# Rounding's last product and its stores on GpSimd, raw weights by SyncE, a PReLU share on ScalarE, four v products per block

## The chip, the cores and the metric

One core of a Trainium2 chip runs the kernel. The metric is the device time of one execution in microseconds (us); the program runs once per measurement, and lower is better.

## What is computed

Talking-heads attention on 4 blocks of 448 tokens with 12 heads, then a two-layer MLP with PReLU on the 1792 tokens that come out. The MLP's weights come as float64 and are rounded to float32 on the chip.

```python
scores = scale * np.matmul(q, k.transpose(0, 1, 3, 2))
scores = np.einsum('bhij,hg->bgij', scores, w_pre)
scores = scores - np.max(scores, axis=-1, keepdims=True)
attn = np.exp(scores)
attn = attn / (np.sum(attn, axis=-1, keepdims=True) + 1e-09)
attn = np.einsum('bhij,hg->bgij', attn, w_post)
x = np.matmul(attn, v).transpose(0, 2, 1, 3).reshape(B * S, H * D)
h = x @ w_in
out = (np.maximum(h, 0.0) + alpha * np.minimum(h, 0.0)) @ w_out
```

## The kernel before, in words

**Attention in steps.** The 448 query rows of a block (one of four batches of tokens) are cut into seven chunks of 60 rows and one of 30 (chunk 7). A chunk is cut into groups of 10 rows by 12 heads; two groups make a step, 90 steps in all, of which steps -1 to 26 are called the lead here. Step n issues, in this order (`step`, from line 567): the mixing of the scores over heads, `mix(n)` (L207), with the row maximum on VectorE (L209); SyncE's relays, copies from SBUF to SBUF that lay the scores of a coming step out by heads (L197, and L200 for the 30-row chunk, which needs twice as many), three steps ahead, into six buffers that a mixing must have read before; `norm(n-1)` on VectorE; a v product if one is due; `post(n-2)`, the second mixing, with 56 small matmuls (L240); the exponentials on ScalarE (L216); the q-k products of a later chunk (L179).

**v products.** `pv` (L263) multiplies the finished attention columns of one or two chunks by v in two halves, for each with 3 x 4 x 2 x 2 matmuls (less the empty ones, 84), evicts with a ScalarE copy (L269) and a VectorE addition (L270), and stores to the scratch `x2` in DRAM (L273). `PVS` lists the chunks of each batch: five per block before. A batch comes LAG + 1 = 3 steps behind its last group. There is one buffer per half of v; the next block's v is loaded when the last batch of a block is issued (L169, L170).

**Conversion.** `convert` (from line 287) rounds the float64 weights in 64 units of 128x384. `round_f64` (from line 50) has five VectorE operations per unit: the exponent's bits (L60), the mantissa's high part (L64), adding the low word (L65), the sign (L66) and the product (L67); GpSimd clamps and scales the exponent between (L61, L62). The last two operations of a unit are issued after the first three of the next. GpSimd fetches the raw words of unit i + 4 when unit i is through (L295, four buffers); the rounded unit is stored to the scratch `wsc` by SyncE (L305), a step later, by `flush`, which runs twice per step. The lead issues 6 of these operations per step, the steps after it 9 until all are done.

**MoE.** When a block's x is whole, `split_x` loads it (L450) and splits each of six tiles into two float32r parts on VectorE (L460, L461). `moe` runs the two layers in pairs of 128-wide pieces, paced by `moe_work` between the attention's operations; weights come back from `wsc` (L338), are split by a ScalarE cast (L346) and a GpSimd subtraction (L347), and multiplied (L400, L434). `prelu` evicts a piece with two VectorE operations (L354, L355), a ScalarE cast (L360) and a subtraction (L361); `add_out` sums the second layer on VectorE (L367, L369). The first block of MoE runs from step 27 on beside the rest of the conversion.

Every engine works through its own list in order, so an instruction that waits holds all that stand behind it on that engine.

Of the kernel before, what the change touches and what calls it, by code (L numbers as in the profile page):

```python
# [70 lines left out]
def talking_heads_prelu(ctx: ExitStack, tc: tile.TileContext, q, k, v, w_pre, w_post, mask, w_in, w_out, alpha, out):  # L71
# [182 lines left out]
    def pv(i, hx):  # L254
        b, r0, cn, base, _, nh = pvs[i]
        to = grab()
        for cl in range(3):
# [9 lines left out]
        dst = xe[:, :3 * cn].rearrange("p (c i u) -> p c i u", i=HI, u=nh)  # L267
        src = to[:, :, :3 * cn].rearrange("p r (c u i) -> p r c i u", i=HI, u=nh)
        nc.scalar.copy(dst, src[:, 0])  # L269
        nc.vector.tensor_tensor(dst, src[:, 1], dst, ALU.add)  # L270
        free(to)
        skip = max(0, 420 - r0) if r0 > 360 else 0
        later.append(lambda: nc.sync.dma_start(  # L273
            out=x2[3 * hx:3 * hx + 3, :, b * S + r0 + skip:b * S + r0 + cn].rearrange("c p i -> p c i"),
            in_=xe[:, :3 * cn].rearrange("p (c i) -> p c i", c=3)[:, :, skip:]))

# [10 lines left out]
    def convert():  # L287
        todo = [(f, x, c) for f in range(NFC) for x in range(2) for c in range(0, DM, CU)]
        raw_c = {}

        def fetch_c(i):
            if i < len(todo):
                f, x, c = todo[i]
                raw_c[i] = cvp.tile([128, CU], I64, tag="cr", bufs=4, name=f"cr{f}_{x}_{c}")
# [382 lines left out]
```

## Time and profile before

| what | us |
| --- | --- |
| median of 3 runs | 998.38 (993.72 to 1003.52) |
| the profiled execution | 997.95 |
| its span | 996.1 |
| TensorE busy in the span | 870.4 (87%) |
| VectorE busy | 622.5 (62%) |
| ScalarE busy | 427.2 (43%) |
| GpSimd busy | 488.3 (49%) |

The span runs from the first to the last instruction of the profiled execution. A busy share is a mean over stages: the lead up to 207 us, the first MoE block beside the conversion up to 389 us, and from there MoE and attention on TensorE. The granted clock is TensorE's, as a share of its higher level (2.4 GHz; the lower is 1.2).

### The profile page before, as it was taken

The page shows a single profiled execution, that of the slowest core. Times are in us where ns is not written, and L with a number is a line of the kernel's source. Part 1 is how long each engine was busy: PE and PEld are TensorE (multiplying, and loading weights), DVE is VectorE, ACT ScalarE, POOL GpSimd, SP SyncE. Part 2 cuts the span into 40 slices and gives each one's busy share as a digit, 9 for nine tenths or more (in the row PEclk, how much of TensorE's full clock was granted, in tenths as well). Part 3 has the DMA queues.
Part 4 walks back from the last instruction along what each step waited for, and adds up shares of the span by engine and source line. Part 5 has one row for each costly group of instructions (what it writes and reads, how often), then busy time and mean ns, then how long its engine had stood idle before and what let it go on. Part 6 is the DMA issues. An engine that isn't in the chain of part 4 may idle for free. (4 is left out here: it accounts for less than half of the span.)

```text
span 996.1 us, 28867 instructions
## 1 busy us (share of the span) xinstructions
PE 870.4 (87%) x12204; PEld 677.2 (68%) x12204; DVE 622.5 (62%) x1077; ACT 427.2 (43%) x780; POOL 488.3 (49%) x562
## 2 busy tenths in 40 slices
PE   6687667596897885997999989999999999999997
PEld 2354435464774763875777866877787888879997
DVE  3699766588799798554544445555654464654564
ACT  1466455243334342453554545443645454232231
POOL 6555534547556753452435424550633334467661
PEclk7799988787898897997999989999999999999999
DMA  7788968746666964464544554465534433544322
GB/s 182 242 255 250 249 184 266 246 144 195 191 181 188 260 188 137 132 195 135 152 122 134 139 122 134 126 176 190 156 119 120 125 99 92 155 130 124 111 80 72
DMA packets 79729, 161.81 MB, mean 162 GB/s; under 512 B 26276, under 2 KB 64304, under 8 KB 79600
## 3 DMA queue, kind: packets, MB, share of 16 engines
q0 software_dynamic: 21312, 90.58, 33.4%
q1 hardware_dynamic: 57432, 68.18, 20.9%
q8 instruction: 96, 1.57, 0.7%
q10 hardware_dynamic: 856, 1.21, 0.5%
q14 instruction: 33, 0.27, 0.1%
HBM read 97.62 MB, written 23.59 MB: 122 GB/s over the span
## 5 line engine op out<-in xcount | busy, mean ns | idle before, releaser
L347 POOL TENSOR_TENSOR ws<-wr,ws 128x768 fp32r<-128x768 f32 x128 | 237.2, 1854 | 300.0 <-ACT ws L346 297.9
L434 PE MATMUL p<-g,ws 128*128 128x448 f32 x1152 | 258.1, 379 | 16.9 <-ACT e L216 7.9
L400 PE MATMUL p<-xs,ws 128*128 128x448 f32 x1152 | 258.0, 377 | 5.2 <-DVE xs L460 3.7
L434 PEld LDWEIGHTS p<-g,ws 128*128 128x128 f32 x1152 | 221.5, 195 | 55.5 <-ACT e L216 9.6
L400 PEld LDWEIGHTS p<-xs,ws 128*128 128x128 f32 x1152 | 216.9, 192 | 48.5 <-issue 13.4
L209 DVE TENSOR_REDUCE nm<-p 128x2 f32<-128x896 f32 x90 | 97.6, 1084 | 105.3 <-PE p L207 105.1
L246 ACT COPY at<-p 128x960 f32<-128x960 f32 x88 | 86.7, 985 | 173.1 <-PE p L240 173.0
L216 ACT ACTIVATE e<-p,nm 128x448 f32<-128x448 f32 x180 | 112.6, 634 | 99.7 <-DVE nm L209 66.9
L240 PEld LDWEIGHTS p<-r,e 64*64 64x64 f32 x5040 | 105.7, 140 | 71.6 <-issue 43.7
L346 ACT CAST ws<-wr 128x768 fp32r<-128x768 f32 x128 | 103.9, 843 | 91.4 <-issue 58.5
L240 PE MATMUL p<-r,e 64*64 64x60 f32 x5040 | 111.1, 227 | 33.0 <-issue 12.2
L179 PE MATMUL p<-k,q 64*64 64x448 f32 x768 | 107.9, 606 | 34.8 <-DVE t L355 15.2
L369 DVE TENSOR_TENSOR acc<-p,acc 128x896 f32<-128x896 f32 x84 | 90.9, 1086 | 70.5 <-PE p L434 69.2
L207 PE MATMUL p<-sr,wk 64*64 64x448 f32 (+1 forms) x720 | 106.0, 596 | 16.5 <-DMA sr<-st 12.2
L354 DVE TENSOR_SCALAR t<-p,alpha_sb 128x448 f32<-128x448 f32 x64 | 43.4, 678 | 98.7 <-PE p L400 98.7
L263 PEld LDWEIGHTS p<-at,v 64*64 64x64 f32 x3360 | 88.0, 138 | 23.5 <-issue 19.6
L263 PE MATMUL p<-at,v 64*64 64x120 f32 (+2 forms) x3360 | 89.3, 253 | 12.8 <-DMA v<-in_v_dram 7.8
L183 ACT COPY st<-p 128x896 f32<-128x896 f32 x95 | 84.1, 913 | 34.2 <-DMA sr<-st 18.4
L338 POOL DMA_DIRECT2D wr<-wsc x128 | 72.2, 564 | 39.9 <-POOL ws L347 35.3
L207 PEld LDWEIGHTS p<-sr,wk 64*64 64x64 f32 (+1 forms) x720 | 26.7, 141 | 58.2 <-issue 28.6
L179 PEld LDWEIGHTS p<-k,q 64*64 64x64 f32 x768 | 28.3, 143 | 54.5 <-ACT st L183 18.1
L61 POOL TENSOR_SCALAR ce<-ce 128x384 int32<-128x384 int32 x64 | 34.4, 537 | 52.5 <-DVE ce L60 50.5
(47 smaller groups left out, 670.9 us busy)
## 6 DMA issues: line engine op xcount, KB each, us to landing
wr<-wsc POOLq DMA_DIRECT2D x128, 384.0 KB, 3.9
sr<-st SPq DMA_DIRECT2D x332, 105.0 KB
cr<-in_w_in_dram POOLq DMA_DIRECT2D x32, 384.0 KB, 5.0
cr<-in_w_out_dram POOLq DMA_DIRECT2D x32, 384.0 KB, 5.5
wsc<-ct SPq DMA_DIRECT2D x64, 192.0 KB
xr<-x SPq DMA_DIRECT2D x24, 224.0 KB
out_dram<-acc SPq DMA_DIRECT2D x12, 448.0 KB
q<-in_q_dram POOLq DMA_DIRECT2D x54, 90.0 KB, 4.9
```

Of the source, the lines that this page charges most:

```text
L179: nc.tensor.matmul(pt[64 * cc:64 * cc + 64, r, :S], q_t[ci][h, (3 * cc + p) * cn + SR0 * cc:(3 * cc + p) * cn + SR0 * cc + 64], k_t[b, p][ ...
L207: nc.tensor.matmul(to[hf:hf + 64, u, :S], wk[r, :], g[r, :], start=True, stop=True)
L209: nc.vector.tensor_reduce(out=nm, in_=to[:, :, :S], axis=AX.X, op=ALU.max, negate=True)
L216: nc.scalar.activation(out=e_t[n][:, u], in_=m_t[n][:, u, :S], func=AF.Exp, bias=nm_t[n][:, u:u + 1], scale=1.0, accum_out=se_t[n][:, u:u ...
L240: nc.tensor.matmul(dst[:, :, HI * u:HI * u + HI], e[h, u, 64 * jb:64 * jb + 64], r[h, u].rearrange("p (h i) -> p h i", h=H), start=True, s ...
L246: nc.scalar.copy(at[:, :, col:col + 2 * GI].rearrange("p q (g i) -> p g q i", g=2), pt[:, :, :NS * GP].rearrange("p g (q i) -> p g q i", i ...
L263: nc.tensor.matmul(to[64 * t:64 * t + 64, r, cl * cn:(cl + 1) * cn], v_t[b, hx][pr, s, (2 * cl + t) * D:(2 * cl + t + 1) * D], a_t[pr, s, ...
L346: nc.scalar.copy(t[:, 0], w)
L347: nc.gpsimd.tensor_tensor(t[:, 1], w, t[:, 0], ALU.subtract)
L369: nc.vector.tensor_tensor(dst, pt[:, :, :N], dst, ALU.add)
L400: nc.tensor.matmul(pt[:, f % 2, :S], w[:, tw, c * 128:(c + 1) * 128], xs[:, tx, c, :], start=(j == 0), stop=(j == 3 * NCC - 1))
L434: nc.tensor.matmul(pt[:, d, :S], w[:, tw, (c + d) * 128:(c + d + 1) * 128], g[:, tg], start=(j == 0), stop=(j == 3 * FG - 1))
```

## The change

- `PVS` has four batches per block: chunks (0, 1), (2, 3), (4, 5), (6, 7) in blocks 0 and 2 and (7, 0), (1, 2), (3, 4), (5, 6) in blocks 1 and 3. A batch that holds chunk 7 has 90 columns, and since its two chunks have different halves it is evicted in two runs, each with a copy, an addition and a store.
- The last operation of the rounding runs on GpSimd for units 0 to 33 and, after these, for units of `w_in`; GpSimd then stores the unit itself. The other 16 units stay on VectorE with a store by SyncE.
- After the first four fetches the raw words are fetched by SyncE, by way of `flush`, once the fourth operation of the unit that held the buffer is issued. `flush` stands behind the step's relays now, and runs once per step (twice before the steps in which a block is ready).
- A lead step issues 5 operations instead of 6 and a later one 8 instead of 9; a GpSimd unit has four.
- In the first block ScalarE does the negative half of `prelu` (Relu of -h, then times -alpha) and the cast of `split_x`.
- The loads of q for chunks 2 and 3 and of the first v stand some steps apart.

```diff
-PVS = [((0, 1), (2, 3), (4,), (5, 6), (7,)), ((7,), (0, 1), (2, 3), (4, 5), (6,))] * 2
-READY = (4, 9, 14, 19)
+PVS = [((0, 1), (2, 3), (4, 5), (6, 7)), ((7, 0), (1, 2), (3, 4), (5, 6))] * 2
+READY = (3, 7, 11, 15)
...
-CONV_LEAD, CONV_T0 = 6, 9
+CONV_LEAD, CONV_T0 = 5, 8
+POOL_UNITS = 34
...
-    yield lambda: v.tensor_tensor(tf, tf, e.bitcast(F32), ALU.mult)
+    yield lambda: last.tensor_tensor(tf, tf, e.bitcast(F32), ALU.mult)
...
+        by_pool = lambda i: i < POOL_UNITS or todo[i][1] == 0
+
+        def fetch_c(i, dma=nc.gpsimd):
...
-                nc.gpsimd.dma_start(out=raw_c[i], in_=(w_in, w_out)[x][f, :, c:c + CU])
+                dma.dma_start(out=raw_c[i], in_=(w_in, w_out)[x][f, :, c:c + CU])
...
-            for j, op in enumerate(round_f64(nc, raw, e, t)):
+            for j, op in enumerate(round_f64(nc, raw, e, t, nc.gpsimd if by_pool(i) else nc.vector)):
                 op()
+                if j == 3:
+                    ripe.append((step_now[0], lambda: fetch_c(i + 4, nc.sync)))
+                    if by_pool(i):
+                        continue
                 if j == 4:
-                    ripe.append((step_now[0], lambda: (stored.add((f, x, c)), nc.sync.dma_start(
-                        out=wsc[f, :, x * DM + c:x * DM + c + CU], in_=t.bitcast(F32)))))
-                    fetch_c(i + 4)
+                    if by_pool(i):
+                        store(nc.gpsimd)
+                    else:
+                        ripe.append((step_now[0], lambda: store(nc.sync)))
...
-            nc.vector.tensor_scalar(out=h, in0=pt[:, f % 2, :S], scalar1=0.0, scalar2=alpha_sb[:, f:f + 1], op0=ALU.min, op1=ALU.mult)
+            if t == 0:
+                nc.scalar.activation(out=h, in_=pt[:, f % 2, :S], func=AF.Relu, scale=-1.0)
+                nc.scalar.mul(h, h, nalpha[:, f:f + 1])
+            else:
+                nc.vector.tensor_scalar(out=h, in0=pt[:, f % 2, :S], scalar1=0.0, scalar2=alpha_sb[:, f:f + 1], op0=ALU.min, op1=ALU.mult)
...
-            nc.vector.tensor_copy(xs[:, 0, c, :], xr[:, :N])
+            (nc.scalar.copy if t == 0 else nc.vector.tensor_copy)(xs[:, 0, c, :], xr[:, :N])
...
-            flush(n - 1)
             if live(n):
                 mix(n)
             if n >= 0:
                 relays(2 * (n + RA + 1), (nc.sync,))
+            flush(n - 1)
```

GpSimd's list in the lead, from unit 5 on, before; `ce` and `ct` are a unit's two buffers, `cr` the raw words, the numbers behind a name are piece, matrix, column and buffer:

```order
L61 TENSOR_SCALAR ce1_0_384_409<-ce1_0_384_409 128x384
L62 TENSOR_SCALAR ce1_0_384_409<-ce1_0_384_409 128x384
L295 DMA cr2_0_0_475<-in_w_in_dram 128x384
L61 TENSOR_SCALAR ce1_1_0_477<-ce1_1_0_477 128x384
L62 TENSOR_SCALAR ce1_1_0_477<-ce1_1_0_477 128x384
L295 DMA cr2_0_384_540<-in_w_in_dram 128x384
L61 TENSOR_SCALAR ce1_1_384_542<-ce1_1_384_542 128x384
L62 TENSOR_SCALAR ce1_1_384_542<-ce1_1_384_542 128x384
L295 DMA cr2_1_0_605<-in_w_out_dram 128x384
```

And after, the same units:

```order
L62 TENSOR_SCALAR ce1_0_384_406<-ce1_0_384_406 128x384
L63 TENSOR_SCALAR ce1_0_384_406<-ce1_0_384_406 128x384
L68 TENSOR_TENSOR ct1_0_0_397<-ct1_0_0_397,ce1_0_0_396 128x384
L320 DMA wsc_58<-ct1_0_0_397 128x384
L62 TENSOR_SCALAR ce1_1_0_477<-ce1_1_0_477 128x384
L63 TENSOR_SCALAR ce1_1_0_477<-ce1_1_0_477 128x384
L68 TENSOR_TENSOR ct1_0_384_407<-ct1_0_384_407,ce1_0_384_406 128x384
L320 DMA wsc_58<-ct1_0_384_407 128x384
L62 TENSOR_SCALAR ce1_1_384_542<-ce1_1_384_542 128x384
L63 TENSOR_SCALAR ce1_1_384_542<-ce1_1_384_542 128x384
```

The fetch is gone from between the units; in its place stand the product `ct<-ct,ce` of the unit before and its store.

SyncE's list from the end of the start-up, before; `sr` are the relays' buffers, `st` the scores of a chunk:

```order
L197 DMA sr5_122<-st0_193 60x1x448 x2
L305 DMA wsc_58<-ct0_0_0_241 128x384
L305 DMA wsc_58<-ct0_0_384_248 128x384
L305 DMA wsc_58<-ct0_1_0_280 128x384
L197 DMA sr0_117<-st1_238 60x1x448 x2
L197 DMA sr1_118<-st1_238 60x1x448 x2
L197 DMA sr2_119<-st1_238 60x1x448 x2
L197 DMA sr3_120<-st1_238 60x1x448 x2
L197 DMA sr4_121<-st1_238 60x1x448 x2
L197 DMA sr5_122<-st1_238 60x1x448 x2
L305 DMA wsc_58<-ct0_1_384_323 128x384
```

And after:

```order
L205 DMA sr5_123<-st0_194 60x1x448 x2
L310 DMA cr1_0_0_292<-in_w_in_dram 128x384
L205 DMA sr0_118<-st1_231 60x1x448 x2
L205 DMA sr1_119<-st1_231 60x1x448 x2
L205 DMA sr2_120<-st1_231 60x1x448 x2
L205 DMA sr3_121<-st1_231 60x1x448 x2
L205 DMA sr4_122<-st1_231 60x1x448 x2
L205 DMA sr5_123<-st1_231 60x1x448 x2
L310 DMA cr1_0_384_347<-in_w_in_dram 128x384
L310 DMA cr1_1_0_349<-in_w_out_dram 128x384
L205 DMA sr0_118<-st2_271 60x1x448 x2
L205 DMA sr1_119<-st2_271 60x1x448 x2
```

The three stores ahead of the twelve relays of chunk 1 (`st1`) have become one fetch, and two fetches stand behind the twelve.

VectorE's list in step 26, before; `xe` is what a v product is evicted to:

```order
L209 TENSOR_REDUCE nm26_2517<-p3_131 128x2
L223 TENSOR_SCALAR s125_2523<-se25_2491 128x2
L224 RECIPROCAL s125_2523<-s125_2523 128x2
L227 TENSOR_TENSOR r25_2526<-wq_115,s125_2523 128x120
L270 TENSOR_TENSOR xe5_0_2570<-p2_130,xe5_0_2570 128x90
L270 TENSOR_TENSOR xe5_1_2615<-p0_128,xe5_1_2615 128x90
L67 TENSOR_TENSOR ct7_1_384_2333<-ct7_1_384_2333,ce7_1_384_2332 128x384
L60 TENSOR_SCALAR ce8_0_384_2659<-cr8_0_384_2330 128x384
```

And after:

```order
L217 TENSOR_REDUCE nm26_2445<-p0_129 128x2
L231 TENSOR_SCALAR s125_2455<-se25_2417 128x2
L232 RECIPROCAL s125_2455<-s125_2455 128x2
L235 TENSOR_TENSOR r25_2458<-wq_116,s125_2455 128x120
L61 TENSOR_SCALAR ce8_1_0_2498<-cr8_1_0_2280 128x384
L65 TENSOR_SCALAR ct8_1_0_2499<-cr8_1_0_2280 128x384
L66 SCALAR_TENSOR_TENSOR ct8_1_0_2499<-cr8_1_0_2280,ct8_1_0_2499 128x384
L67 SCALAR_TENSOR_TENSOR ce8_0_384_2423<-cr8_0_384_2195,ce8_0_384_2423 128x384
L61 TENSOR_SCALAR ce8_1_384_2508<-cr8_1_384_2451 128x384
L492 TENSOR_TENSOR xs0_2511<-xr0_0_2437,xs0_2511 128x448
```

The two additions of a v product are gone from the step, and behind the unit's operations the subtractions of `split_x` (`xs<-xr,xs`) stand without the casts.

## Rows read from the trace of the kernel before

**Rows 1.** Stretches: us; busy us (xcount) of PE, PEld, DVE, ACT, POOL; clock; DMA; GB/s.

```profile
59.90:115.80 55.90, 43.90 (x1271) 30.68 (x1268) 52.31 (x116) 35.47 (x72) 30.21 (x52) 0.94 0.87 255
...
207.20:389.10 181.90, 145.23 (x1785) 108.36 (x1785) 160.93 (x265) 70.62 (x128) 114.39 (x147) 0.87 0.65 189
389.10:996.10 607.00, 583.91 (x7410) 482.10 (x7408) 317.79 (x497) 262.38 (x467) 271.68 (x243) 0.98 0.45 131
```

**Rows 2.** Groups by line and shape: the v products on TensorE.

```profile
L263 PE MATMUL p<-at,v 64*64 64x120 f32 x2016 | 62.5, 269 | 0.0
...
L263 PE MATMUL p<-at,v 64*64 64x30 f32 x672 | 14.4, 237 | 10.8 <-DMA v<-in_v_dram 7.8 <-issue 2.1 <-ACT e L216 0.9
...
L263 PE MATMUL p<-at,v 64*64 64x60 f32 x672 | 12.4, 221 | 2.0 <-issue 1.2 <-ACT e L216 0.8
```

**Rows 3.** Timeline, TensorE: post products that stopped; in brackets the idle time before.

```profile
121.04 0.58 PE L240 MATMUL p<-r,e 64*64 64x60 f32 x11 [5.50 <-issue]
...
582.15 0.36 PE L240 MATMUL p<-r,e 64*64 64x60 f32 x2 [2.63 <-issue]
...
673.46 0.28 PE L240 MATMUL p<-r,e 64*64 64x60 f32 x5 [0.90 <-issue]
```

**Rows 4.** Timeline, steps 26 and 27, by several engines.

```profile
182.20 1.03 SPq L450 DMA_DIRECT2D xr<-x  x2
...
186.22 5.18 PE L263 MATMUL p<-at,v 64*64 64x30 f32 x165 [7.79 <-DMA v<-in_v_dram]
...
195.30 0.39 DVE L460 CAST xs<-xr 128x448 fp32r<-128x448 f32 x1
...
196.38 6.86 SPq L450 DMA_DIRECT2D xr<-x  x4
...
200.81 0.40 DVE L460 CAST xs<-xr 128x448 fp32r<-128x448 f32 x1 [3.50 <-DMA xr<-x]
```

**Rows 5.** Groups from 59.9 to 115.8 us, VectorE: the five operations of a unit.

```profile
L66 DVE SCALAR_TENSOR_TENSOR ce<-cr,ce 128x384 int32<-128x384 int32 x14 | 10.2, 732 | 0.0
L65 DVE SCALAR_TENSOR_TENSOR ct<-cr,ct 128x384 f32<-128x384 uint32 x13 | 8.9, 686 | 0.4
L67 DVE TENSOR_TENSOR ct<-ct,ce 128x384 f32<-128x384 f32 x14 | 7.8, 556 | 0.4
L60 DVE TENSOR_SCALAR ce<-cr 128x384 int32<-128x384 int32 x13 | 5.2, 397 | 0.4
L64 DVE TENSOR_SCALAR ct<-cr 128x384 int32<-128x384 int32 x13 | 4.6, 357 | 0.0
```

**Rows 6.** Groups by line and shape: GpSimd's subtraction.

```profile
L347 POOL TENSOR_TENSOR ws<-wr,ws 128x768 fp32r<-128x768 f32 x128 | 237.2, 1854 | 300.0 <-ACT ws L346 297.9
```

**Rows 7.** Groups from 207 to 390 us, VectorE.

```profile
L67 DVE TENSOR_TENSOR ct<-ct,ce 128x384 f32<-128x384 f32 x30 | 28.1, 938 | 0.8
...
L354 DVE TENSOR_SCALAR t<-p,alpha_sb 128x448 f32<-128x448 f32 x12 | 8.1, 676 | 11.5 <-PE p L400 11.5
```

**Rows 8.** Timeline of the start, SyncE's queue, ScalarE and TensorE.

```profile
27.93 7.52 SPq L305 DMA_DIRECT2D wsc<-ct  x3
...
28.12 1.71 ACT L183 COPY st<-p 128x896 f32<-128x896 f32 x2
...
35.55 10.25 SPq L197 DMA_DIRECT2D sr<-st  x12
...
42.15 3.37 PE L207 MATMUL p<-sr,wk 64*64 64x448 f32 x6 [7.63 <-DMA sr<-st]
```

**Rows 9.** Timeline, SyncE's queue around the 30-row chunk.

```profile
125.33 0.33 SPq L305 DMA_DIRECT2D wsc<-ct  x1
...
128.90 7.31 SPq L200 DMA_DIRECT2D sr<-st  x8
```

**Rows 10.** Timeline, a step's mixing on TensorE and its reduction on VectorE.

```profile
66.03 0.92 PE L207 MATMUL p<-sr,wk 64*64 64x448 f32 x8
...
69.45 1.07 DVE L209 TENSOR_REDUCE nm<-p 128x2 f32<-128x896 f32 x1
```

More of the change, by code (lines that the diff above doesn't have):

```diff
@@ L46, with round_f64 @@
 CU = DM // 2
-CONV_LEAD, CONV_T0 = 6, 9
-def round_f64(nc, raw, e, t):
+CONV_LEAD, CONV_T0 = 5, 8
+POOL_UNITS = 34
+def round_f64(nc, raw, e, t, last):
     w = raw.bitcast(I32).rearrange("p (n t) -> p n t", t=2)
@@ L88, in talking_heads_prelu @@
         for cs in lists:
-            r0 = CHUNKS[cs[0]][0]
-            cn = sum(CHUNKS[cs[-1]]) - r0
-            base = AW - cn if lists[-1] == cs == (len(CHUNKS) - 1,) else 0
+            cn = sum(CHUNKS[c][1] for c in cs)
+            base = AW - cn if lists[-1] == cs and len(CHUNKS) - 1 in cs else 0
+            runs, o = [], 0
             for c in cs:
-                a_col[place[b, c]] = base + CHUNKS[c][0] - r0
-            pvs.append((b, r0, cn, base, lb[place[b, cs[-1]]], half(place[b, cs[0]])))
+                ci = place[b, c]
+                a_col[ci] = base + o
+                if runs and runs[-1][3] == half(ci) and runs[-1][4] + runs[-1][1] == CHUNKS[c][0]:
+                    runs[-1][1] += CHUNKS[c][1]
+                else:
+                    runs.append([o, CHUNKS[c][1], max(0, 420 - CHUNKS[c][0]) if c == len(CHUNKS) - 1 else 0, half(ci), CHUNKS[c][0]])
+                o += CHUNKS[c][1]
+            pvs.append((b, runs, cn, base, lb[place[b, cs[-1]]]))
     pv_at = {p[4] + LAG + 1: i for i, p in enumerate(pvs)}
@@ L123, in talking_heads_prelu @@
     alpha_sb = cst.tile([128, NFC], F32, name="alpha_sb")
+    nalpha = cst.tile([128, NFC], F32, name="nalpha")
     wk = cst.tile([128, 64], F32, name="wk")
@@ L254, in pv @@
     def pv(i, hx):
-        b, r0, cn, base, _, nh = pvs[i]
+        b, runs, cn, base, _ = pvs[i]
         to = grab()
@@ L266, in pv @@
         xe = xep.tile([128, 3 * AW], F32, tag="xe", name=f"xe{i}_{hx}")
[L267 to L270, printed above, removed]
+        for o, w, skip, nh, r0 in runs:
+            if w == cn:
+                dst = xe[:, :3 * cn].rearrange("p (c i u) -> p c i u", i=HI, u=nh)
+                src = to[:, :, :3 * cn].rearrange("p r (c u i) -> p r c i u", i=HI, u=nh)
+                s0, s1 = src[:, 0], src[:, 1]
+            else:
+                dst = xe[:, :3 * cn].rearrange("p (c n) -> p c n", c=3)[:, :, o:o + w].rearrange("p c (i u) -> p c i u", i=HI)
+                s0, s1 = (to[:, r, :3 * cn].rearrange("p (c n) -> p c n", c=3)[:, :, o:o + w].rearrange("p c (u i) -> p c i u", i=HI)
+                          for r in range(2))
+            nc.scalar.copy(dst, s0)
+            nc.vector.tensor_tensor(dst, s1, dst, ALU.add)
         free(to)
[L272 to L275, printed above, removed]
+        for o, w, skip, nh, r0 in runs:
+            later.append(lambda o=o, w=w, skip=skip, r0=r0: nc.sync.dma_start(
+                out=x2[3 * hx:3 * hx + 3, :, b * S + r0 + skip:b * S + r0 + w].rearrange("c p i -> p c i"),
+                in_=xe[:, :3 * cn].rearrange("p (c i) -> p c i", c=3)[:, :, o + skip:o + w]))
     ripe = []
@@ L316, in convert @@
             seq += [(i, 0), (i, 1), (i, 2)] if i < n else []
-            seq += [(i - 1, 3), (i - 1, 4)] if i else []
+            seq += [(i - 1, 3)] + ([] if by_pool(i - 1) else [(i - 1, 4)]) if i else []
         units = {}
@@ L322, in convert @@
             next(units[i], None)
+            if i < 2 and j == 1:
+                fetch_c(i + 2)
             yield
@@ L539, in talking_heads_prelu @@
         next(conv)
-        for ci in (2, 3):
-            load_q(ci)
         conv_done, conv_steps = 0, NFC * 2 * 5 * (DM // CU)
@@ L576, in step @@
             step_now[0] = n
-            if n == 1:
-                for hx in range(2):
-                    load_v(0, hx)
+            if n in (0, 1):
+                load_q(n + 2)
+            if n in (2, 3):
+                load_v(0, n - 2)
             due = pv_at.get(n)
@@ L616, in step @@
                 converts(CONV_T0 - CONV_T0 // 2)
-            flush(n - 1)
+            if n + 1 in ready:
+                flush(n - 1)
             for t in range(len(TB)):
@@ L625, in step @@
                     nxt_x[0] = iter(())
+            if n == 4:
+                nc.vector.tensor_scalar(out=nalpha, in0=alpha_sb, scalar1=-1.0, scalar2=None, op0=ALU.mult)
             if n == ready[0] - 5:
```

10 lines of the change are left out of this document (7 added, 3 removed).

## The prediction

> **What bounds the kernel now.** I read the table of stretches first, because the kernel has three stages with different limits. From 59.9 to 115.8 us, in the lead, VectorE is busy 52.3 of 55.9 us and TensorE only 43.9; from 207.2 to 389.1, the first MoE block with the rest of the conversion, VectorE has 160.9 of 181.9 and TensorE runs at 0.87 of its clock; from 389.1 on TensorE is busy 583.9 of 607.0 us at 0.98, and nothing else matters [rows 1]. So there are two questions: what the change takes from VectorE's queue, and from the waits ahead of TensorE, before 389 us; and what it takes from TensorE itself after that. Then I read the groups by shape for the price of a v product, the groups of the two VectorE-bound stretches for the price of a unit, and the timeline where TensorE stands still.
>
> The profiled execution took 997.95 us (span 996.1, 1.85 us around it); the sum is made against it. The median of the three runs, 998.38, is 0.4 us higher. One per cent, 10 us, is about what a measurement of this kernel can tell from no change.
>
> **v products, five batches per block of tokens to four.** A batch is 168 matmuls at any width. Twelve batches of 120 columns kept TensorE busy 62.5 us, so 5.2 us each; four of 60 columns 12.4, so 3.1; four of 30 columns 14.4, so 3.6 [rows 2]. After, twelve of 120 stay and four of 90 replace the eight narrow ones. The trace has no 90-column batch: it costs between 3.1 and 5.2 us, and I take the middle, 4.1. The saving is 4 x (3.1 + 3.6 - 4.1) = 10.4 us (6 to 14). What counts for the end lies after 389 us: there ran 7 wide, 3 of 60 and 2 of 30 columns (52.9 us); now 7 wide and 2 of 90 (44.6), so -8.3.
>
> A narrow batch has a second price. In three places TensorE stopped just behind one, in the middle of the post products, with no releaser but "issue": 5.50 us in the lead, 2.63 and 0.90 later, with one of 1.47 between these two [rows 3]. After 389 us the timeline shows none of this kind behind a 120-column batch. I expect the later three, 5.0 us, to go, as a 90-column batch goes through its instructions more slowly than a narrow one (4.1 against 3.1 us). After 389 us: -8.3 - 5.0 = **-13.3** (-5 to -19).
>
> **Step 26.** Its v product waited 7.79 us for v of block 1, since the 30-column piece of block 1 comes one step after that of block 0 and there is one v buffer; VectorE, in order, stood behind it, and the first split of x began at 195.30 although its two x loads were issued at 182.20 [rows 4]. Now the first batch of block 1 (chunks 7 and 0) comes three steps later, step 26 has no v product, and VectorE's list of that step loses both additions. A later x load was issued at 196.38 and used at 200.81, so 4.4 us: the first split can begin at 182.2 + 4.4 = 186.6, 8.7 us earlier. The remaining splits are bound by loads; six casts at 0.39 us go to ScalarE beside that and bring perhaps 1 us, and the wider batch in step 25 costs 0.9. **-9** (-3 to -14).
>
> **The rounding's last operation in the lead.** VectorE loses 0.556 us per unit of 2.73 (0.732 + 0.686 + 0.556 + 0.397 + 0.357) [rows 5]; 2.17 stay. A step has five operations of four per unit, 1.25 units, where it had six of five, 1.2. GpSimd gains a two-input product. The trace has it at twice the width, 1.854 us [rows 6]; half of that, 0.93, is the lower end, the whole the upper; I take 0.95, as only the fixed part does not halve. GpSimd was idle 25.7 of 55.9 us there, so the time itself is covered. What is not covered is VectorE: its operations on SBUF grow while GpSimd works. The same product on VectorE took 0.556 us here, where GpSimd does short operations, and 0.938 in the first block, where it does the 1.85 us subtractions [rows 5, 7]. So a GpSimd operation can hold VectorE for some of its length: between 0 and 0.95 us for each new product. By VectorE's order, three of five products start while the next VectorE operation reads SBUF twice or fast, two while the reduction from PSUM runs; 0.6 x 0.95 = 0.57. A step of VectorE then changes by 1.25 x (2.17 + 0.57) - 1.2 x 2.73 = +0.15 us; 22 steps make **+3** (-12 to +13).
>
> The Trainium skill, "SBUF — State Buffer", section "SBUF: two separate sides", speaks against this part: VectorE and GpSimd share a port pair that one of them holds for a whole instruction, and the other fully blocks. The trace agrees in direction, 0.938 against 0.556 us. By the rule at its hardest every product would cost its full length; that is a rival below.
>
> **Raw weights fetched by SyncE.** A fetch now stands behind the relays of the step after the one that freed its buffer. SyncE issues a relay in 0.85 us (12 in 10.25), a store in 0.33 [rows 8, 9]. Behind SyncE's four relays the fetch leaves 3.4 + 0.4 us after the step's mixing, and lands some 4.4 us later [rows 4]: 8.2 us after it. By the order, in steps 2, 6, 10, 14, 18, 22 and 26 VectorE wants it as the last operation of that very step, with the next step's reduction behind. In the VectorE-bound stretch TensorE has mixed about 2.5 us before the reduction (66.03 + 0.92 against 69.45) [rows 10], and VectorE needs some 4 us more to reach the fetch: 6.5 against 8.2, so 0 to 4.5 us late, mostly about 1. I take **+5** for the lead (0 to +31).
>
> At the start nothing is won by it. Three stores kept SyncE from 27.93 to 35.45 and the next 12 relays left only at 35.55, though ScalarE's copies were done at 29.83; TensorE waited 7.63 us [rows 8]. Now no store is ahead, the relays run from 30 to 40, but unit 5's fetch is behind all twelve, lands near 45, and the next reduction waits for it as it did: **-1** (-6 to +2).
>
> Around 120 to 155 us SyncE is the limit, eight relays of the 30-row chunk per step in 7.31 us; a store that waited for VectorE from 125.33 on let them begin only at 128.90 [rows 9]. That 3.5 us goes, part of the 5.50 us stop goes, and the eight-relay steps now delay a fetch: **-5** (-10 to +8).
>
> **First block.** VectorE loses 12 operations at 0.676 in this stretch (8.1 us) and 15 products at 0.938 (14.1) [rows 7]; the 15 on GpSimd hold it 15 x 0.57 = 8.6, and late fetches, up to one per step, cost perhaps 3: 8.1 + 14.1 - 8.6 - 3 = 10.6. ScalarE takes two operations of some 0.6 us for each of 16 tiles; it was busy 70.6 of 181.9 us [rows 1], which covers them. **-10.6** (+5 to -20).
>
> **Sum.** -1 + 3 + 5 - 5 - 9 - 10.6 - 13.3 = -30.9; 997.95 - 30.9 = 967 us.
>
> **Rivals.** *The shared port costs in full.* Each of the 48 products on GpSimd holds VectorE its whole 0.95 us: 48 x 0.38 = 18 us more, 985. For it: 0.938 against 0.556. Against it: in the lead GpSimd's short operations left the product at 0.556.
>
> *The early waits are refilled.* VectorE or SyncE is relieved, but a transfer or TensorE at 0.87 of its clock is next; the terms -5 and -9 are lost, 981. For it: stops around 120 us lie in a stretch with heavy transfers. Against it: step 26 waited for one named load.
>
> *Port and fetch cost little.* Lock 0.28 instead of 0.57 (-14) and no fetch late (-8): 945. For it: SyncE is freed of waits on VectorE, so it can run ahead.
>
> *Slower: the fetch is late everywhere.* One mechanism, the place behind the relays: seven times 4.5 us in the lead (31.5 instead of 5) and 2 us in each of 15 steps of the first block (30 instead of 3): +53, 1020. By the order some 20 units of the first block, too, are wanted in the step in which their fetch is issued. It outweighs all gains once the 27 tight places cost 39 / 27 = 1.45 us each. Against it: SyncE no longer waits for VectorE's product.
>
> **How the numbers follow.** Forecast 0.52, port in full 0.12, refilled 0.12, little cost 0.15, late fetch 0.09. The forecast's own range is 952 to 984; with the two dearer cases to 994 and two thirds of the cheap one to 941 the range leaves out some 0.14. Faster by over 1% (under 988): nearly all of the forecast and the cheap case, 0.09 of "refilled" and 0.07 of "port": 0.82. Within 1%: 0.11, the upper ends of these two and a mild late fetch. Slower: 0.07.
>
> **What would show it.** Right: 2688 v-product matmuls; no wait for v in step 26, first x split near 185; the first block near 170 us with VectorE still its busiest elementwise engine; from there to the end 590 to 600 us; GpSimd's product at 0.9 to 1.1 us, VectorE's operations behind it longer by about half of that. Wrong: VectorE idle before the unit's first operation for a raw-weight load by more than 15 us in all (late fetch), unit operations growing by 0.9 us per product (port), or TensorE's time after the first block unchanged.

## The result, and where the time went

| kernel | us, median | ratio to before, 95% interval |
| --- | --- | --- |
| before | 1000.25 (4 runs) | |
| after | 1015.02 (1012.23 to 1019.32) | 1.0143, 1.0099 to 1.0187 |
| forecast | 967 (941 to 994) | |

The change made the kernel 1.4% slower, where the forecast had it 31 us faster. The profiled execution of after took 1015.54 us, 17.6 more than the one of before. The start of a step's reduction on VectorE (line 217) cuts both traces into the stretches of the prediction:

| stretch | before | after | measured | forecast |
| --- | --- | --- | --- | --- |
| to step 3 | 46.0 | 56.2 | +10.2 | -1 |
| steps 3 to 25 | 135.6 | 143.1 | +7.5 | +3 (3 + 5 - 5) |
| step 26 | 25.6 | 23.9 | -1.7 | -9 |
| first block, steps 27 to 41 | 181.9 | 190.7 | +8.8 | -10.6 |
| from step 42 to the end | 607.0 | 599.7 | -7.3 | -13.3 |
| sum | 996.1 | 1013.6 | +17.5 | -30.9 |

Only the last stretch got shorter. The table of stretches of after says where to look (columns as in [rows 1]):

```profile
59.90:115.80 55.90, 42.22 (x1028) 29.46 (x1028) 48.45 (x98) 32.86 (x64) 39.06 (x59) 0.87 0.70 220
223.20:413.90 190.70, 151.83 (x1953) 116.56 (x1954) 138.68 (x236) 85.34 (x157) 117.05 (x142) 0.88 0.60 182
413.90:1013.60 599.70, 577.30 (x6913) 475.60 (x6911) 313.10 (x492) 266.23 (x473) 273.02 (x245) 0.98 0.46 132
```

VectorE was the busy engine of the first two stretches before: 94% and 88%. Now it is busy 87% of the first, cut alike, and 73% of the second, which is longer. Less work, more time: VectorE waits for something new. Its waits, from 24 to 210 us and then from 200 to 420 (what it waited for, us in total, times, longest), name it:

```profile
DVE ce L61 <- DMA cr<-in_w_in_dram: 23.8, 4, 16.4
DVE ce L61 <- DMA cr<-in_w_out_dram: 15.4, 4, 8.8
...
DVE t L386 <- ACT t L383: 31.8, 11, 8.3
DVE ce L61 <- DMA cr<-in_w_out_dram: 10.6, 2, 8.8
```

Raw weights: 23.8 + 15.4 = 39.2 us up to 210 us, where VectorE idled 4.5 us ahead of this operation before, and 8.8 more in step 26, the longer of the two in the last row. ScalarE's half of the activation: 31.8 us in the first block, a wait that did not exist before. How long a wait is does not yet say what it costs; the experiments below price both. The longest of the first kind is at the start; this is SyncE's queue, ScalarE and VectorE there in after, to be read beside [rows 8]:

```profile
23.80 0.37 SPq L310 DMA_DIRECT2D cr<-in_w_in_dram  x1
34.54 10.32 SPq L205 DMA_DIRECT2D sr<-st  x12
44.97 0.45 SPq L310 DMA_DIRECT2D cr<-in_w_in_dram  x1
...
33.60 1.72 ACT L191 COPY st<-p 128x896 f32<-128x896 f32 x2
...
39.05 0.55 DVE L67 SCALAR_TENSOR_TENSOR ce<-cr,ce 128x384 int32<-128x384 int32 x1
55.95 0.36 DVE L61 TENSOR_SCALAR ce<-cr 128x384 int32<-128x384 int32 x1 [16.35 <-DMA cr<-in_w_in_dram]
56.23 1.08 DVE L217 TENSOR_REDUCE nm<-p 128x2 f32<-128x896 f32 x1
```

SyncE stood idle from 24.2 to 34.5, waiting for the scores that the first relay copies: by the program's order the last of chunk 1's three copies from PSUM is the first of the two at 33.60, done at 34.51. Then it issued twelve relays, and only then the fetch that VectorE wanted at 39.6. It left at 44.97 and VectorE could go on at 55.95, 11 us later. The stretches around three late fetches, those that VectorE used at 55.95, 181.46 and 213.42 (columns as above), and around two that took about 5 us from issue to use:

```profile
45.00:56.00 11.00, 4.03 (x8) 0.66 (x6) 0.05 (x1) 0.00 (x0) 1.98 (x4) 0.66 0.96 252
172.00:181.00 9.00, 2.06 (x16) 0.60 (x8) 0.67 (x2) 0.95 (x1) 3.41 (x6) 0.69 0.99 331
205.00:214.00 9.00, 0.00 (x0) 0.00 (x0) 0.58 (x2) 1.13 (x2) 5.09 (x9) 0.62 0.95 292
73.00:78.00 5.00, 5.00 (x156) 3.68 (x147) 1.07 (x3) 2.19 (x3) 4.16 (x7) 1.00 0.83 248
144.00:149.00 5.00, 3.46 (x79) 2.08 (x73) 1.03 (x2) 1.68 (x2) 3.48 (x5) 1.00 0.82 259
```

In the first three the DMA engines are busy 95 to 99% of the time. TensorE, VectorE and ScalarE stand for most of it, and GpSimd's busy time there is in part the issuing of loads and stores: the fetch shares the DMA engines with these and with the relays issued ahead of it. TensorE's granted clock is 0.62 to 0.69 there.

Step 26, of which the forecast expected 9 us, in after (ScalarE, then TensorE):

```profile
207.93 0.56 ACT L491 CAST xs<-xr 128x448 fp32r<-128x448 f32 x1 [5.29 <-DMA xr<-x]
209.23 0.56 ACT L491 CAST xs<-xr 128x448 fp32r<-128x448 f32 x1 [0.74 <-DMA xr<-x]
216.90 0.56 ACT L491 CAST xs<-xr 128x448 fp32r<-128x448 f32 x1 [7.10 <-DMA xr<-x]
...
222.08 0.56 ACT L491 CAST xs<-xr 128x448 fp32r<-128x448 f32 x1 [0.89 <-DMA xr<-x]
222.55 0.97 ACT L254 COPY at<-p 128x960 f32<-128x960 f32 x1
...
223.58 2.98 PE L431 MATMUL p<-xs,ws 128*128 128x448 f32 x7 [18.83 <-ACT at L254]
```

The wait for v of [rows 4] is gone. In its place ScalarE waits, in order, for one x load after the other, and the copy of the attention result (line 254), which frees the PSUM pair that TensorE needs, stands behind the last of them.

### The profile page after: what moved, and what is told of

Read it like the earlier page. It is cut to its first block, busy times and chain, and to the rows that moved or that the text cites. A ratio compares the mean times of both kernels' runs of the same rounds, so it can differ in the third digit from the quotient of the medians.

```text
span 1013.6 us, 27492 instructions
## 1 busy us (share of the span) xinstructions
PE 863.7 (85%) x11532; PEld 677.3 (67%) x11532; DVE 589.6 (58%) x1008; ACT 449.7 (44%) x818; POOL 529.5 (52%) x598
## 5 line engine op out<-in xcount | busy, mean ns | idle before, releaser
L465 PE MATMUL p<-g,ws 128*128 128x448 f32 x1152 | 254.7, 376 | 12.4 <-POOL ws L374 6.2
L248 PEld LDWEIGHTS p<-r,e 64*64 64x64 f32 x5040 | 109.2, 144 | 105.9 <-issue 66.3
L187 PE MATMUL p<-k,q 64*64 64x448 f32 x768 | 112.5, 622 | 27.6 <-DVE t L386 12.9
L215 PE MATMUL p<-sr,wk 64*64 64x448 f32 (+1 forms) x720 | 102.7, 586 | 8.3 <-DMA sr<-st 7.1
L271 PEld LDWEIGHTS p<-at,v 64*64 64x64 f32 x2688 | 78.7, 136 | 15.5 <-ACT e L224 9.8
L271 PE MATMUL p<-at,v 64*64 64x120 f32 (+1 forms) x2688 | 80.6, 266 | 7.5 <-ACT e L224 7.4
L385 DVE TENSOR_SCALAR t<-p,alpha_sb 128x448 f32<-128x448 f32 x48 | 32.6, 679 | 80.0 <-PE p L431 80.0
L68 POOL TENSOR_TENSOR ct<-ct,ce 128x384 f32<-128x384 f32 x48 | 49.9, 1039 | 38.2 <-DVE ce L67 36.7
L386 DVE SCALAR_TENSOR_TENSOR t<-p,t 128x448 f32<-128x448 f32 x64 | 39.9, 624 | 46.0 <-ACT t L383 44.3
L61 DVE TENSOR_SCALAR ce<-cr 128x384 int32<-128x384 int32 x64 | 30.8, 482 | 57.8 <-DMA cr<-in_w_in_dram 30.7
```

The source lines that it names most:

```text
L187: nc.tensor.matmul(pt[64 * cc:64 * cc + 64, r, :S], q_t[ci][h, (3 * cc + p) * cn + SR0 * cc:(3 * cc + p) * cn + SR0 * cc + 64], k_t[b, p][ ...
L215: nc.tensor.matmul(to[hf:hf + 64, u, :S], wk[r, :], g[r, :], start=True, stop=True)
L248: nc.tensor.matmul(dst[:, :, HI * u:HI * u + HI], e[h, u, 64 * jb:64 * jb + 64], r[h, u].rearrange("p (h i) -> p h i", h=H), start=True, s ...
L271: nc.tensor.matmul(to[64 * t:64 * t + 64, r, cl * cn:(cl + 1) * cn], v_t[b, hx][pr, s, (2 * cl + t) * D:(2 * cl + t + 1) * D], a_t[pr, s, ...
L465: nc.tensor.matmul(pt[:, d, :S], w[:, tw, (c + d) * 128:(c + d + 1) * 128], g[:, tg], start=(j == 0), stop=(j == 3 * FG - 1))
```

## The experiments

Two theories: **A**, the place of the raw fetch behind the relays is the loss; **B**, ScalarE's share is. Two smaller ones: **C**, GpSimd's product stops VectorE; **D**, the eviction of a v product in two runs holds TensorE up. Each kernel was timed beside the kernel before.

### A: where the raw weights are fetched

After, with the fetch back on GpSimd:

```diff
-                    ripe.append((step_now[0], lambda: fetch_c(i + 4, nc.sync)))
+                    fetch_c(i + 4)
```

> The changed kernel, with one edit: the raw weights of unit i+4 are fetched on GpSimd's queue at once behind operation 3 of unit i, as before the change, and not by SyncE behind the next step's relays. Theory A (the late fetch is the loss): VectorE's waits for a raw tile, 39.2 us of its time between 25 and 200 us in the changed kernel, fall under 8 us, step 27's reduction starts near 207 us instead of 223.2, and the kernel takes 995 to 1002 us. Theory B (ScalarE's part of the activation and of the casts is the loss): the first steps get shorter by at most 5 us, and the kernel takes 1010 to 1015 us. Theory C (the product on GpSimd stops VectorE): the waits go, but the operations on VectorE stay slow, and no more than half of the 16 us comes back, 1006 to 1010 us.

998.91 us, 0.9995 of before (0.9953 to 1.0036): 16 us back, as A said. The waits fell to 9.3 us, a little over the bound; step 27 begins at 213.2, not at 207. The rest of the lead stayed long, by 6 us against before: GpSimd now spends 0.58 us on each fetch, ahead of its product. The trace has a likely reason, which no run of its own tests: the later product falls on other operations of VectorE (under C), and the two of `norm` at lines 231 and 235 take 1.08 us per step from 60 to 180 us, against 0.75 in the next kernel, over 22 steps some 7 us.

After, with the fetch on SyncE but the queue's waiting transfers ahead of the relays:

```diff
+            flush(n - 1)
             if live(n):
                 mix(n)
             if n >= 0:
                 relays(2 * (n + RA + 1), (nc.sync,))
-            flush(n - 1)
```

> The changed kernel, with one edit: what has waited for SyncE since the last step (fetches and stores) is issued at the head of a step, ahead of the step's relays, and not behind them. The fetch stays on SyncE. If the place behind the relays makes the fetch late: the waits for raw tiles between 25 and 200 us fall from 39 us to under 10, and the kernel takes 996 to 1004 us. If a transfer on SyncE's queue lands late wherever it is issued (8 to 11 us from issue to use): at least half of the waits stay, and the kernel takes 1008 to 1016 us. The relays begin about 0.6 us later for each transfer ahead of them, which in either case gives back 0 to 4 us.

989.80 us, 0.9884 of before (0.9853 to 0.9914), 25 us below after and better than either theory's range. The start in this kernel, SyncE and VectorE:

```profile
23.94 9.83 SPq L310 DMA_DIRECT2D cr<-in_w_in_dram  x2
...
36.28 10.76 SPq L205 DMA_DIRECT2D sr<-st  x12
...
39.52 0.35 DVE L61 TENSOR_SCALAR ce<-cr 128x384 int32<-128x384 int32 x1
48.12 1.09 DVE L217 TENSOR_REDUCE nm<-p 128x2 f32<-128x896 f32 x1 [8.24 <-PE p L215]
```

The same fetch left by 33.8 us, while SyncE had nothing to relay, and VectorE did not wait for it; the relays began 1.7 us later, behind one more fetch. The reduction then waits 8.24 us for TensorE, as it did before the change: the stop at the start is that of the relays again. Step 27 begins at 205.6 (223.2 in after), and the first block takes 182.3 us (190.7). Waits for raw tiles are still 17.5 us up to 210 us, more than expected, and single fetches still took up to 13 us from issue to use; yet the lead is 1.6 us shorter than before. The longest wait, 6.7 us at 195.85, lies in step 26, where the x loads are next.

The other direction, the kernel before with nothing but the late fetch:

```diff
                 if j == 4:
-                    fetch_c(i + 4)
+                if j == 3:
+                    late.append((step_now[0], lambda: fetch_c(i + 4, nc.sync)))
...
                 relays(2 * (n + RA + 1), (nc.sync,))
+            flush_late(n - 1)
```

> The kernel before with one edit: raw weights are fetched by SyncE behind the relays of the next step, as in the change, and everything else stays. Theory A (this place alone makes the loss): VectorE waits 25 us or more for raw tiles up to 200 us (4.5 us before), the start of step 27 moves from 207 to 217 us or later, the block gets longer, and the kernel takes 1012 to 1030 us. Rival (the place is a loss only with the other parts, since the conversion before is slower by its products): 998 to 1006 us.

1022.14 us, 1.0261 of before (1.0185 to 1.0337). VectorE's waits for raw tiles up to 210 us:

```profile
DVE ce L60 <- DMA cr<-in_w_out_dram: 21.7, 9, 5.9
...
DVE ce L60 <- DMA cr<-in_w_in_dram: 6.1, 5, 2.8
```

27.8 us instead of 4.5; step 27 at 215.6, slightly short of what was expected, and the first block 193.2 us (the profiled execution is the fastest of the four, 1016.38 us). The loss lies elsewhere here: the start is no longer than before (step 3 at 44.3 us), the waits up to 210 us are many and short, and the first block is 11.3 us longer. With the other parts of the change or without them, this one place costs 23 to 25 us. A holds.

### B: ScalarE's share

After, with activation and casts on VectorE:

```diff
-            if t == 0:
+            if False:
...
-            (nc.scalar.copy if t == 0 else nc.vector.tensor_copy)(xs[:, 0, c, :], xr[:, :N])
+            nc.vector.tensor_copy(xs[:, 0, c, :], xr[:, :N])
```

> The changed kernel, with the first block's activation and the casts of its x back on VectorE alone. Theory B (VectorE and TensorE wait for ScalarE's half): VectorE's waits for it, 30.4 us in the first block, and step 26's stop of 18.8 us on TensorE for the attention copy behind the casts go; the block gets 5 to 10 us shorter and the kernel takes 1003 to 1009 us. Theory A alone (the block waits for late raw weights, and ScalarE's half is a gain of 8 us): the block gets longer by what VectorE has to do again, 48 operations of some 0.7 us, of which a half to all counts, and the kernel takes 1015 to 1035 us.

1004.22 us, 1.0059 of before (1.0027 to 1.0091): 11 us below after, B's case. VectorE does more, and the block takes 182.4 us instead of 190.7. This diff joined to that of the transfers ahead of the relays:

> The kernel with SyncE's waiting transfers ahead of the relays (989.8 us), and the first block's activation and the casts of x back on VectorE alone. Theory B (ScalarE's half is a loss on its own): the first block, 182.3 us from step 27 to step 42, gets 5 to 10 us shorter, and the kernel takes 979 to 985 us. Rival (what the share cost in the changed kernel, 11 us, was a late fetch felt twice, and without late fetches ScalarE's half pays): the block gets 0 to 10 us longer, 990 to 1000 us.

978.98 us, 0.9801 of before (0.9768 to 0.9834), again 11 us, now without late fetches: A and B add. The block takes 173.8 us. To part the two shares, this kernel with the casts alone on ScalarE, so that against after the edits are the head of the step and one line:

```diff
-            if t == 0:
+            if False:
```

> The kernel with SyncE's waiting transfers ahead of the relays and the first block's activation back on VectorE (979 us with the casts back too, 989.8 us with neither back); the casts of x stay on ScalarE. If the 11 us that ScalarE's share costs come from the activation (VectorE waits 31 us in 12 times for it in the block): 977 to 981 us, and the block from step 27 to step 42 takes 172 to 176 us. If they come from the casts (TensorE's stop of 15.5 us in step 26, for the attention copy behind the casts on ScalarE): 985 to 990 us.

987.20 us (0.9888, 0.9842 to 0.9934): 8.2 of the 10.8 us are the casts'. The 2.6 us left for the activation are not clear of the scatter (its interval and that of 989.8 us overlap), so the largest row of the waits, 31.8 us, is worth little or nothing. Step 26 with the casts on VectorE, the kernel of 979 us (ScalarE, then TensorE):

```profile
189.40 0.98 ACT L254 COPY at<-p 128x960 f32<-128x960 f32 x1 [0.73 <-PE p L248]
207.42 0.63 ACT L224 ACTIVATE e<-p,nm 128x448 f32<-128x448 f32 x1 [17.04 <-DVE s L231]
...
195.07 2.64 PE L431 MATMUL p<-xs,ws 128*128 128x448 f32 x6 [2.71 <-DVE xs L491]
200.71 2.90 PE L431 MATMUL p<-xs,ws 128*128 128x448 f32 x6 [3.00 <-DVE xs L491]
204.27 6.03 PE L431 MATMUL p<-xs,ws 128*128 128x448 f32 x15 [0.66 <-DVE xs L491]
```

and with them on ScalarE:

```profile
206.90 0.56 ACT L491 CAST xs<-xr 128x448 fp32r<-128x448 f32 x1 [0.25 <-DMA xr<-x]
207.37 0.97 ACT L254 COPY at<-p 128x960 f32<-128x960 f32 x1
...
208.39 7.79 PE L431 MATMUL p<-xs,ws 128*128 128x448 f32 x24 [14.86 <-ACT at L254]
```

In the first the copy is done at 190.4, and TensorE begins the block at 195.07 and takes each piece of x as it comes; in the second it starts at 208.39 with all six. Step 26 lasts about the same (20.9 and 21.4 us); the time shows up in the block behind it, 173.8 against 179.9. That the casts cost by their place ahead of that copy is read from these rows; a kernel with the casts on ScalarE behind the copy was not run.

### C: the product on GpSimd

```diff
-            for j, op in enumerate(round_f64(nc, raw, e, t, nc.gpsimd if by_pool(i) else nc.vector)):
+            for j, op in enumerate(round_f64(nc, raw, e, t, nc.vector)):
```

In the kernel of 989.8 us:

> The kernel with SyncE's waiting transfers ahead of the relays (989.8 us), and the last rounding operation back on VectorE for all units; its store stays on GpSimd's queue, the order stays. Theory C as predicted (a product of 1.04 us on GpSimd stops VectorE for 0.45 us and saves it 0.65): VectorE's other operations get their times of before back, the lead gets 0 to 8 us longer and the kernel takes 988 to 998 us. Rival (the stops cost more than the product saves, since a whole operation waits for the lock): the lead gets 3 to 10 us shorter, 980 to 987 us.

988.67 us (0.9904, 0.9874 to 0.9935). In the kernel of 979 us:

> The kernel of 979 us, with the last rounding operation back on VectorE in all units; stores and order stay. The block takes 173.8 us in it and 184.3 us in the kernel with the v products alone, which differ in the product's engine, the store's queue, the fetch's queue and the pace. If the product is the cause: 985 to 990 us, block 181 to 185 us. If the queues and the pace are: 978 to 982 us, block 174 to 177 us.

981.32 us (0.9836, 0.9780 to 0.9892), with a block of 172.5 us. One is 1.1 us faster with the product on VectorE, the other 2.3 slower, and the intervals overlap in both pairs: the product's engine makes no difference that these runs can tell. The groups from 60 to 116 us suggest why. With the product on GpSimd (the kernel of 989.8 us), to be read beside [rows 5]:

```profile
L65 DVE TENSOR_SCALAR ct<-cr 128x384 int32<-128x384 int32 x14 | 11.7, 834 | 0.0
L67 DVE SCALAR_TENSOR_TENSOR ce<-cr,ce 128x384 int32<-128x384 int32 x14 | 9.2, 660 | 0.0
L66 DVE SCALAR_TENSOR_TENSOR ct<-cr,ct 128x384 f32<-128x384 uint32 x13 | 7.7, 593 | 0.4
L61 DVE TENSOR_SCALAR ce<-cr 128x384 int32<-128x384 int32 x14 | 6.2, 443 | 0.6 <-DMA cr<-in_w_out_dram 0.6
...
L68 POOL TENSOR_TENSOR ct<-ct,ce 128x384 f32<-128x384 f32 x14 | 14.3, 1020 | 6.6 <-DVE ce L67 6.0
```

and on VectorE:

```profile
L67 DVE SCALAR_TENSOR_TENSOR ce<-cr,ce 128x384 int32<-128x384 int32 x15 | 10.1, 671 | 0.0
L68 DVE TENSOR_TENSOR ct<-ct,ce 128x384 f32<-128x384 f32 x14 | 8.4, 597 | 0.5
L66 DVE SCALAR_TENSOR_TENSOR ct<-cr,ct 128x384 f32<-128x384 uint32 x14 | 8.3, 596 | 0.4
L65 DVE TENSOR_SCALAR ct<-cr 128x384 int32<-128x384 int32 x14 | 5.1, 365 | 0.0
L61 DVE TENSOR_SCALAR ce<-cr 128x384 int32<-128x384 int32 x14 | 4.9, 353 | 1.1 <-DMA cr<-in_w_out_dram 1.1
```

The other four operations take 0.834 + 0.660 + 0.593 + 0.443 = 2.53 us beside GpSimd's product and 0.671 + 0.596 + 0.365 + 0.353 = 1.98 without it. By these four, a product of 1.02 us on GpSimd holds VectorE for 0.55 us on average, most of it in the operation of line 65, and saves it 0.60. The average hides two cases. This product began 0.1 us ahead of line 65 (GpSimd, then VectorE, the kernel of 989.8 us; the last row is line 66 in the kernel with the fetch on GpSimd, beside a product from 80.32 to 81.33):

```profile
61.23 1.04 POOL L68 TENSOR_TENSOR ct<-ct,ce 128x384 f32<-128x384 f32 x1 [2.16 <-DVE ce L67]
...
61.34 1.15 DVE L65 TENSOR_SCALAR ct<-cr 128x384 int32<-128x384 int32 x1
...
80.01 1.75 DVE L66 SCALAR_TENSOR_TENSOR ct<-cr,ct 128x384 f32<-128x384 uint32 x1
```

Eight of the 14 operations of line 65 meet a product and take 1.15 to 1.17 us; the other six, which meet none, take 0.35 to 0.52. The row maximum keeps its 1.07 us beside a product. Lines 66 and 67 meet none here; where line 66 does, as in the last row, it takes 1.75 us instead of 0.56. So what a product costs depends on the operation that it meets: summed from 60 to 180 us over all operations that overlap a product, 0.60 us per product in the kernel of 989.8 us and 0.96 with the fetch on GpSimd, against the 0.60 that it saves. The rest of the units on GpSimd too, in the kernel of 979 us:

```diff
-POOL_UNITS = 34
+POOL_UNITS = 64
```

> The kernel of 979 us (SyncE's transfers ahead of the relays, no share for ScalarE), with the last rounding operation and the store on GpSimd in all 64 units, and not in 48 or so. If a product on GpSimd is a gain where VectorE is the busy engine: the block gets another 1 to 4 us shorter, 975 to 978 us. If the lock or GpSimd's queue makes it a loss there: 980 to 985 us.

982.32 us (0.9842, 0.9795 to 0.9889), no gain: the block takes 182.7 us, not 173.8, and the stretch behind it 590.0, not 595.8, which was not taken apart. In the block VectorE now waits 10.3 us, six times, for GpSimd's line 63 (5.8 us, twice, in the kernel of 979 us): the product stands ahead of these short operations in GpSimd's queue.

### D: the v products

The kernel before with the four batches and their eviction alone; all other parts (conversion, fetch, flushes, activation, casts, start) are those of before:

```diff
-PVS = [((0, 1), (2, 3), (4,), (5, 6), (7,)), ((7,), (0, 1), (2, 3), (4, 5), (6,))] * 2
-READY = (4, 9, 14, 19)
+PVS = [((0, 1), (2, 3), (4, 5), (6, 7)), ((7, 0), (1, 2), (3, 4), (5, 6))] * 2
+READY = (3, 7, 11, 15)
```

> The kernel before with the four batches of v products and their evictions alone; conversion, fetches, flushes, activation, casts and start stay as before. If the gain behind the first block (607 us from step 42 to the end before, 598 in all variants of the change) is that of the batches alone: the stretch takes 597 to 600 us and the kernel 986 to 994 us. If part of it came from the conversion that is off VectorE and SyncE by then: 601 to 606 us there, and 995 to 1000 us in all.

988.65 us, 0.9897 of before (0.9864 to 0.9931). The stretch behind the first block takes 595.6 us instead of 607.0, a little shorter than expected: the gain there is the batches'.

After, with both copies of an eviction ahead of both additions:

```diff
-            nc.vector.tensor_tensor(dst, s1, dst, ALU.add)
+            adds.append((dst, s1))
+        for dst, s1 in adds:
+            nc.vector.tensor_tensor(dst, s1, dst, ALU.add)
```

> The changed kernel, where the eviction of a v product of two runs makes both ScalarE copies first and then both VectorE additions (now: copy, addition, copy, addition, and the second copy waits for the first addition). Theory D (this exchange between the two engines holds TensorE up): the second copy no longer waits (9.5 us of ScalarE's waits for an addition go), TensorE's stops of 9.1, 4.75 and 4.39 us at 243, 320 and 389 us shrink by half or more, and the kernel takes 1004 to 1010 us. Rival: VectorE is late with the first addition for other reasons, and the second copy's wait only stands in place of the same wait later: 1013 to 1016 us.

1009.60 us (1.0085, 1.0055 to 1.0114). The time is in D's range, but TensorE's waits for the additions from 230 to 420 us hardly shrank (the line has moved to 288):

```profile
PE p L248 <- DVE xe L288: 16.9, 3, 8.6
```

18.2 us in after (three times, the longest 9.1), although the second copy's wait for the first addition is gone. This diff joined to the kernel of 979 us:

> As the kernel before it in this batch, and the evictions of two runs make both copies ahead of both additions. Theory D (the exchange costs about 5 us wherever it stands, as from 1015.0 to 1009.6 us): 4 to 6 us below the kernel without this edit, 974 to 981 us. Rival (the 5 us were ScalarE's, which has less to do here): within 2 us of it.

979.74 us (0.9813, 0.9773 to 0.9852): nothing, the rival's case. Where VectorE is late, it is late with the first addition as well; D falls as a cost of its own. What the 5 us in after were stays open; the intervals of 1009.6 and 1015.0 us overlap, so they may be scatter.

### The parts together

| kernel, each with one part more than the last | us | step |
| --- | --- | --- |
| before | 998.4 | |
| + four v products per block of tokens | 988.7 | -9.8 |
| + fetch on SyncE ahead of the relays, store on GpSimd, new start, pace and flushes | 981.3 | -7.3 |
| + product on GpSimd | 979.0 | -2.3 |
| + casts of the first x on ScalarE | 987.2 | +8.2 |
| + first block's activation shared | 989.8 | +2.6 |
| + transfers behind the relays (after) | 1015.0 | +25.2 |

The parts of the second step were not taken apart, and the steps of 2.3 and 2.6 us are within the scatter. The medians are of four batches of runs, with 999.7, 998.4 and 999.0 us for before, and 1000.25 beside after. The version of 979.0 us beats both kernels, by 19 and by 36 us.

## Why the prediction was wrong

**The start, -1 forecast, +10.2 measured.** The step that failed is "unit 5's fetch is behind all twelve, lands near 45, and the next reduction waits for it as it did". The order was read rightly, the row not: the two copies that [rows 8] show done at 29.83 are the second of chunk 1 and the first of chunk 2. The relays need the third of chunk 1, in before the first of these two, done at 33.36:

```profile
32.45 1.71 ACT L183 COPY st<-p 128x896 f32<-128x896 f32 x2
```

So the relays ran from 34.5 to 44.9, not from 30 to 40, and the fetch behind them took 11.0 us and not 4.4 to land. That one wait, 16.35 us, is the largest single piece of the loss.

**The late fetch in the lead, +5 forecast.** The mechanism, and where it would strike, were right: all waits over 2 us lie in steps 2, 6, 18, 22 and 26, five of the seven named. The mis-sized term is the landing time, 4.4 us, taken from one x load of 224 KB. A fetch is 384 KB, and the trace of before had its median from issue to landing (the last figure of these rows), with three between 112.9 and 130.9 us that took 9.7 to 11.0:

```profile
cr<-in_w_in_dram POOLq DMA_DIRECT2D x32, 384.0 KB, 5.0
cr<-in_w_out_dram POOLq DMA_DIRECT2D x32, 384.0 KB, 5.5
```

In after, fetches took about 5 us with the DMA engines 82% busy, and 8 to 11 us in the three places where they were 95 to 99% busy; those three waits, 16.35 + 8.79 + 8.79, make 33.9 of the 48.0 us up to step 27. From step 3 to step 25 the three terms together (+3) measured +7.5.

**The lock, +3 forecast.** Right in size, in part by luck: 0.57 us per product forecast, 0.55 to 0.60 measured, and no effect on the time that the runs can tell. The forecast had three of five products hold VectorE for 0.95 us and two fall on the row maximum; in the kernel of 989.8 us twelve of 14 hold something, eight of them line 65 for 0.8 us, and two fall on the row maximum. As an average, "the shared port costs in full" is excluded there; with the fetch on GpSimd, 0.96 us per product, it came true. By the Trainium skill ("SBUF — State Buffer", section "SBUF: two separate sides") the engine that gets the port pair that VectorE and GpSimd share holds it for a whole instruction, and the other, where it needs the pair, is blocked. The trace comes near that for the operations that a product meets: line 65 took 1.15 us instead of 0.35 beside a product of 1.04.

**SyncE around the 30-row chunk, -5 forecast.** Steps 17 to 19, in which the eight relays are issued, took 24.2 us instead of 25.8; most of the term did not come.

**Step 26, -9 forecast, -1.7 measured.** The wait for v went, and the first cast came 8.6 us after the step's reduction instead of 13.7. Behind it the x loads set the pace, and a raw fetch was late by 8.79 us in the same step. In the kernel of 979 us the step is 4.7 us shorter than before. "Refilled" was the right rival here.

**The first block, -10.6 forecast, +8.8 measured.** The step that failed is "busy 70.6 of 181.9 us, which covers them". ScalarE had the time but not the place: its queue runs in order, the casts in it wait for x loads, and the copy that frees TensorE's pair stands behind them. The subtraction that goes with each cast stayed on VectorE, so VectorE waited for the same loads. Late fetches, put at 3 us, cost 8.4 (190.7 against 182.3). Without both, in the kernel of 979 us, the block is 8.1 us shorter than before. That this is near the forecast is luck: that kernel has no activation on ScalarE (8.1 us of the sum), and with the products back on VectorE (14.1 - 8.6) its block takes 172.5 us, no longer than the 173.8. The v products alone leave it at 184.3, so its gain comes from the new places of fetch and store, the pace and the start together, to which the sum gave nothing and which were not taken apart.

**Behind the first block, -13.3 forecast, -7.3 measured** in after and -11.4 with the v products alone. The groups of after that answer to [rows 2]:

```profile
L271 PE MATMUL p<-at,v 64*64 64x120 f32 x2016 | 64.9, 275 | 7.4 <-ACT e L224 7.4
L271 PE MATMUL p<-at,v 64*64 64x90 f32 x672 | 15.7, 241 | 0.1
```

A 90-column batch takes 15.7 / 4 = 3.9 us (forecast 4.1), the whole 80.6 instead of 89.3. Of the three later stops with "issue" (two of them in [rows 3]) one of 1.07 us is left in after, but there is a new and longer one ahead of post products, with ScalarE's copy of scores as its releaser:

```profile
610.30 1.86 PE L248 MATMUL p<-r,e 64*64 64x60 f32 x54 [5.08 <-ACT st L191]
```

so the 5.0 us put on them did not come: TensorE stands for 599.7 - 577.3 = 22.4 us behind the first block, and stood for 607.0 - 583.9 = 23.1 before. What makes up the 4 us between after and the v products alone was not taken apart.

The rival "the fetch is late everywhere", at 0.09, names the mechanism that happened, with a price of 25 us where 53 were put: the fetch was late in few places, not everywhere. The argument against it, that SyncE no longer waits for VectorE's product, was true and beside the point: SyncE waits for the relays' own conditions, and the fetch waits with it.

From 967 to 1015 us are 48: 25 for the place of the fetch, 11 for ScalarE's share, which no rival named, and 12 by which the kernel of 979 us misses the forecast, most of them at the start and in step 26.

## What to carry to other kernels

A prefetch goes on a queue at the place where its buffer is free, ahead of instructions that still wait for something; behind them it inherits their wait, and here it paid this in a stretch where its own landing time had doubled. Size a transfer's landing from the busiest stretch of the DMA engines, not from one row. Work moved to an engine with idle time is free only if nothing behind it in that engine's queue is waited for: look for the instruction behind it before its busy share. And price a wait by taking it away: with the largest sum of waits here, 31.8 us, only some 2.6 us went.

## What the runs showed that was not expected

In after, with the DMA engines 95 to 99% busy, four 384 KB fetches that VectorE waited for took 8 to 12 us from issue to use, against 4 to 5 at 80 to 85%; this is a tendency and no rule, since two others took 5.6 us at 95 and 99%, one at 127.2 us and one at 268.4. And a product on GpSimd does not slow VectorE evenly: line 65 takes 0.35 us or 1.15, by whether a product runs beside it, the row maximum the same either way, and line 66 kept its time in the kernel of 989.8 us since no product met it. Moving an unrelated issue of 0.58 us ahead of the product changed which operation it met, and with it the price of the product from 0.60 to 0.96 us.
